# The last half gate in a bank of finished attention results, and one row of the mixed product at most behind each gate

## The chip, the cores and the metric

The kernel runs on one core of a Trainium2 chip. The metric is the device time of one execution in microseconds (us); less is better. All numbers come from runs on the chip and from the hardware profile of one execution of the kernel before.

## What is computed

Three stages stand behind each other, all in float32. The weights of the two feed-forward stages come in float64.

```python
def _attn_ref(q, k, v):                       # B, H, S, D = 4, 8, 768, 64
    for t in range(S):
        state = gamma * state + k[:, :, t] (x) v[:, :, t]
        y[:, :, t] = scale * q[:, :, t] @ state
def _moe_ref(x, w1, w2, w3, w_out):           # 3072 tokens, 512 -> 1024 -> 512
    h = (x @ w1) * (x @ w2) @ w3
    return h @ w_out
def _moe2_ref(x, w_in, w_out):                # 512 -> 2048 -> 512
    h = x @ w_in
    return (h * sigmoid(1.702 * h)) @ w_out
```

Since nothing stands between `w3` and `w_out` but a product, the kernel multiplies the two weights once (the "mixed product" `w3 @ w_out`) and applies the result to the gated values.

## The kernel before, in words

**Precision.** Each float32 operand is split into a high and a low part. ScalarE (ACT) casts the high part, VectorE (DVE) subtracts it from the value and keeps the low part. A product is then three matmuls on TensorE (PE), in `mm3`, lines 256 to 259: high by high, high by low, low by high. A "product" of 128 rows and 512 columns over 512 inputs is 12 matmuls of 512 columns.

**Weights.** `weight_steps` (lines 188 to 235) turns the float64 bits of one weight tile after the other into float32 on DVE. It is a generator: one step is one DVE instruction on 128x512 elements. A tile from 2 to 20 has ten steps: two clamps (L194), two subtractions for the low parts of the tile before (L148), two shifts (L202), two ORs (L206) and two more ORs (L216). Behind each L216, ACT casts that half's high part (`upper`, L143), and SyncE (SP) is asked for the next raw weights. Tiles from 21 have eight steps, with no low part. `magnitude` (L139, ACT) opens a tile. `work(n)` (line 243) issues n steps at that place of the program. Tiles 0 to 7 are the gate weights, 8 to 11 `w_out`, 12 to 19 `w3`, 20 to 35 the two weights of the last stage. The `w3` tiles (tag "wc", line 99) have room for two tiles, so the cast of tile 14 writes over tile 12, and so on: the high part of tile 12 + r + 2 can be written only when PE has read tile 12 + r. Each tile from 20 on, and each pair of rows of the mixed product, goes through `seven` (line 177): four TENSOR_TENSOR and three DMAs on GpSimd (POOL). The `x` buffers in which DVE prepares a tile are six halves, three tiles (line 137).

**First stage.** Attention runs in 24 chunks (`Attention.run`). Its results go to PSUM tiles `y0` and `y1`, two banks each, by turns. Between chunks, `fill` puts half gates on PE: one half of a gate product (12 matmuls) into the bank `wide`, named `psg`. Half gate 14 runs in the last chunk, half gate 15 behind attention, in the loop of lines 1026 to 1035, which takes the bank `free[halves % len(free)]`. With 15 % 5 = 0 that is the first of the list. `first_out` copies an even half gate with ACT (L1001) and multiplies an odd one into it with DVE (L1003).

**Second stage.** The loop of lines 1106 to 1136 goes over five blocks of 512 tokens (n = 1 to 5) and eight gates each (t = 0 to 7). A gate (n, t) is 24 matmuls into two banks (`psm`, six banks, so three gates). Then come, in the program's order: for t = 3 to 6 one split of the next block's input (`split_x`, ACT L272 and DVE L173), `work(...)`, the output of the gate (`gate_out`: ACT copies the first half, L299, DVE multiplies by the second, L300), and the rows of the mixed product that line 1123 lets through. A row is again 24 matmuls (`mix_mm`, two banks `psw`), followed by `work(7)` and an ACT copy (`mix_out`, L1066). In blocks 1 and 2 a pair of gates shares one buffer `h` of two, which is stored to DRAM behind the odd gate (L313); at gate (2,6) the other buffer is given to a load (line 1115), so the output of (2,6) needs the buffer whose store holds gates (2,4) and (2,5).

Each engine takes its instructions in the order in which the program issues them, so a waiting instruction holds up all that stand behind it on its engine.

Line 1123 lets a row through while the steps issued so far cover its weights. Before, that gave rows 0 and 1 behind gate (1,5), rows 2 to 4 behind (1,6) and rows 5 to 7 behind (1,7).

Of the kernel before, what the change touches and what calls it, by code (L numbers as in the profile page):

```python
# [24 lines left out]
KD, KF, KG = DM // P, DF // P, DG // P  # L25
# [20 lines left out]
def tile_kernel(  # L46
# [49 lines left out]
    WO, W3, WI = 8, 12, 20  # L96
# [21 lines left out]
    def fetch(held=False, queue=nc.sync):  # L118

        nonlocal fetched  # L120
        if fetched >= min(used + R_BUFS, 2 * len(tiles)):
            return
        i, c = divmod(fetched, 2)
        fetched += 1
        src = tiles[i][0][:, c * WC : (c + 1) * WC].bitcast(I32)
        raw = prep.tile([P, WC, 2], I32, tag="r", bufs=R_BUFS, name="raw")
        if held:
            nc.vector.memset(raw[:, :1], 0)
        queue.dma_start(raw, src.rearrange("p (c w) -> p c w", w=2))
        raws.setdefault(i, []).append(raw)  # L130

    def magnitude(i):
        if i >= len(tiles):
            return
        xs = wx.setdefault(i, [])
        for raw in raws.get(i, [])[len(xs) :]:
            x = prep.tile([P, WC], F32, tag="x", bufs=6, name="x")
            high = raw[:, :, 1].bitcast(F32)
            nc.scalar.activation(x, high, AF.Abs, scale=2.0**16)  # L139
            xs.append(x)  # L140
# [97 lines left out]
    complete = done = 0  # L238
# [4 lines left out]
    def work(n):  # L243

        nonlocal complete, done
        for _ in range(n):
            if done < limit:
                complete = next(steps, len(tiles))
                done += 1

    def weight(i):
        while complete <= i:
            work(1)
        return parts[i]
# [20 lines left out]
    def reload(key, d):  # L275
        lo = x_tiles(key)[1][:, d].bitcast(F32)
        nc.sync.dma_start(
            lo.rearrange("p (c t) -> p c t", c=CPB), xd[key][:, :, d].rearrange("c p t -> p c t")
        )

    def split_x(key, d):
        hi, lo = (t[:, d] for t in xhl[key])
        split(hi, lo, lo.bitcast(F32))

    def gate_half(t, m, key, ps):

        w = [x.rearrange("p (m k f) -> p m k f", m=2, k=KD) for x in weight(t)]
        xh, xl = xhl[key]
        for d in range(KD):
            mm3(ps, w[0][:, m, d], w[1][:, m, d], xh[:, d], xl[:, d], d == 0, d == KD - 1)  # L290
# [11 lines left out]
    def h_tile():  # L302
        return xs.tile([P, 2, TB], F32, tag="h", bufs=2, name="h")
# [562 lines left out]
    def opening(t):  # L866
        if t in range(1, 5):
            load_wm(t - 1)
        if t == 1:
            x = spare.tile([P, 7, TB], F32R, tag="ope", name="h0")  # L870
            hi2[0] = x[:, NM:]
            load_h(0, 0, NM, x[:, :NM])
        if t == KF - 2:
            for k in (0, 2):
                load_h(1, k, k + 2, prep.tile([P, 2, TB], F32R, tag="r", bufs=R_BUFS, name="h1"))
        if t in (3, 4, 5):
            split_h(0, t - 3, t - 2, hi2[0][:, t - 3 : t - 2])
        if t == 6:
            hi2["k3"] = prep.tile([P, TB], F32R, tag="x", bufs=6, name="h3")
            split_h(0, 3, 4, hi2["k3"].rearrange("p (a t) -> p a t", a=1))  # L880
        if t in (4, 6):
            split_wm(t // 2 - 2)
# [79 lines left out]
    with tc.manual_schedule():  # L962
# [4 lines left out]
        with (  # L967
            tc.tile_pool(name="p0", bufs=1, reuse_waits="tile") as p0,
            tc.tile_pool(name="ps0", bufs=1, space=PSUM, reuse_waits="tile") as ps0,
        ):  # L970
            attention = Attention(p0, ps0)
            nc.scalar.activation(still[:, :1], still[:, :1], AF.Copy, scale=0.5)
            attention.load(0)
            nc.gpsimd.dma_start(attention.mask, cmask)
            nc.sync.dma_start(attention.dv, cv)
            nc.sync.dma_start(attention.step[:, :NCK], cstep)
            attention.load(1)
            attention.factors(0)
            for c in range(2, 6):
                attention.load(c)  # L980
            for _ in range(2):
                fetch(queue=nc.gpsimd)
            attention.factors(1)
            halves = 0
            late = []
            wide = ps0.tile([P, TB], F32, name="psg")

            def first_gate(ps):
                nonlocal halves
                t, m = divmod(halves, 2)  # L990
                gate_half(t, m, 0, ps)
                late.append((t, m, ps))
                halves += 1

            def first_out(t, m, ps):
                nonlocal h
                if m == 0 and t % 2 == 0:
                    h = h_tile()
                out = h[:, t % 2]
                if m == 0:  # L1000
                    nc.scalar.copy(out, ps)  # L1001
                    return
                nc.vector.tensor_tensor(out, out, ps, ALU.mult)  # L1003
                if t % 2:
                    nc.sync.dma_start(hd[0][:, t // 2, :2], h)

            def fill(c, at):
                for _ in range((c, at) in ((6, 0), (7, 0), (8, 0))):
                    fetch(held=True)
                if at == 3 and c > 2 * CPB and halves // 2 < min(complete, KF):  # L1010
                    first_gate(wide)
                if at == 0:
                    while late:
                        first_out(*late.pop())
                if at == 1 and c in (*range(2, 6), *range(10, 14)):
                    hi, lo, x = first_x.pop(0)
                    nc.scalar.copy(hi, x)
                    engine = nc.vector if c > 2 * CPB else nc.gpsimd
                    engine.tensor_tensor(lo, x, hi.bitcast(F32), ALU.subtract)
                if c > CPB:  # L1020
                    work(PACE.get(c, (0, 1, 0, 4))[at])
                if (c, at) == (8, 2):
                    magnitude(1)

            attention.run(fill)
            free = [wide] + [
                y[:, j].rearrange("p n t -> p (n t)") for y in attention.y for j in range(2)
            ]
            while late:
                first_out(*late.pop())  # L1030
            while halves < 2 * KF:
                weight(halves // 2)
                first_gate(free[halves % len(free)])
                work(2)
                first_out(*late.pop())
        with (
# [11 lines left out]
            rows = 0  # L1048
# [57 lines left out]
            for n, i in list(enumerate(ORDER))[1:]:  # L1106
                nxt = ORDER[n + 1] if n + 1 < NB else None
                for t in range(KF):
                    if nxt is None:
                        opening(t)  # L1110
                    elif t < 2:
                        for d in range(2):
                            reload(nxt, 2 * t + d)
                    if n == 2 and t == KF - 2:
                        load_b(n, NM, nc.sync)
                    if n == 3 and t == 0:
                        load_b(n, 1, nc.sync)
                    ab = gate_mm(t, i, gate_tile)
                    if nxt is not None and t in range(KD - 1, KF - 1):
                        split_x(nxt, t - KD + 1)  # L1120
                    work(((8, 6, 3, 3)[n - 1] + (n < 4) * (t % 2)) if n < 5 else (t < 4) + (t < 5))
                    (gate_second if n > 2 else gate_first)(t, i, ab)
                    while rows < KF and (complete > W3 + rows or (n, t) == (2, KF - 1)):
                        ps = mix_mm(rows)
                        work(7)
                        mix_out(rows, ps)
                        rows += 1
                        if rows == KF:
                            stage.close()
                            pb = homes["st"] = stage.enter_context(  # L1130
                                tc.tile_pool(name="b2", bufs=1, reuse_waits="tile")
                            )
                            st_ready = [pb.tile([P, 1024], F32, tag="st", bufs=2, name="st")]
                            pb.tile([P, 2048], F32, name="gap")
                            first_g = [g_tile()]
                            first_b = [b12_tile()]
# [148 lines left out]
```

## Time and profile before

| what | value |
| --- | --- |
| median of 3 runs | 968.72 us (968.15 to 969.56) |
| the profiled execution: its own time | 968.64 us |
| its span, first to last instruction | 966.8 us |
| PE busy | 947.2 us, 98% |
| DVE busy | 705.6 us, 73% |
| ACT busy | 432.2 us, 45% |
| POOL busy | 226.8 us, 23% |
| granted TensorE clock, mean | 0.999 |
| chain that ended last, PE's share | 89% |

Busy time is the sum of an engine's instructions; matmuls overlap, so PE's share says how rarely it stands still, not how fast it is. The clock was at its upper level throughout. Time outside the span (1.8 us) is start and end of the program. The second stage of the product described above runs from 128.8 to 391 us of the span.

### The profile page before, as it was taken

The numbers are of one execution on the slowest core, as the hardware profiler recorded it, in microseconds if no ns is written. First come the engines' busy times: TensorE is split into PE (matmuls) and PEld (weight loads), VectorE is DVE, ScalarE is ACT, GpSimd is POOL, SyncE is SP. The second block draws the span as 40 slices with busy tenths as digits, with TensorE's granted clock in tenths as the row PEclk, the third lists the DMA queues.
The fourth block names the chain that finished last, engine by engine and source line by source line (L and its number), as shares of the span: only waits on it lengthen the run. The fifth ranks groups of instructions, "written<-read, shape, count | busy, mean of one in ns | idle before, by whom it ended". The sixth has DMA issues, their size and how long they took to land.

```text
span 966.8 us, 14667 instructions
## 1 busy us (share of the span) xinstructions
PE 947.2 (98%) x5656; PEld 781.6 (81%) x5656; DVE 705.6 (73%) x857; ACT 432.2 (45%) x643; POOL 226.8 (23%) x281
## 2 busy tenths in 40 slices
PE   6899999999999999999999999999999999999998
PEld 5687777888888888888888888888888888888886
DVE  5898878988899887675795776568586665566662
ACT  4554435433313212645436665556545544353430
POOL 7422100379787866240010000000000000000000
PEclk9999999999999999999999999999999999999999
DMA  9999765579998999799867845754987867766761
GB/s 351 390 356 347 279 216 197 193 243 341 343 351 318 364 322 405 281 326 340 276 227 265 307 165 219 297 207 185 324 314 279 330 230 258 253 217 231 278 230 54
DMA packets 90646, 268.52 MB, mean 278 GB/s; under 512 B 7536, under 2 KB 15984, under 8 KB 82512
## 3 DMA queue, kind: packets, MB, share of 16 engines
q1 hardware_dynamic: 74592, 188.60, 55.0%
q0 software_dynamic: 15840, 78.91, 21.3%
q8 instruction: 44, 0.72, 0.3%
q14 instruction: 26, 0.21, 0.1%
q10 hardware_dynamic: 144, 0.07, 0.0%
HBM read 166.37 MB, written 101.19 MB: 277 GB/s over the span
## 4 chain that ended last, share of the span: by engine, by line
PE 89%; DMA 4%; DVE 3%; ACT 1%; issue 1%; POOL 0%; DVEq 0%; ACTq 0%; POOLq 0%; SPq 0%
PE m L257 12%; PE m L259 12%; PE m L258 12%; PE psm L258 6%; PE psm L257 6%; PE psm L259 6%; PE a L257 4%; PE a L258 4%; PE a L259 4%; PE e L258 2%; PE e L257 2%; PE e L259 2%; DMA qkv<-in_qkv_dram 2%; PE psg L257 2%; DMA raw<-in_w_dram 1%; PE psw L259 1%
## 5 line engine op out<-in xcount | busy, mean ns | idle before, releaser
L257 PE MATMUL psm<-xh,wh 128*128 128x512 f32 x320 | 124.5, 389 | 0.0
L258 PE MATMUL psm<-xl,wh 128*128 128x512 f32 x320 | 124.5, 389 | 0.0
L259 PE MATMUL psm<-xh,wl 128*128 128x512 f32 x320 | 124.5, 389 | 0.0
L257 PE MATMUL m<-h,op 128*128 128x512 f32 x320 | 124.5, 389 | 0.0
L259 PE MATMUL m<-h,op 128*128 128x512 f32 x320 | 124.5, 389 | 0.0
L258 PE MATMUL m<-l,op 128*128 128x512 f32 x304 | 118.3, 389 | 0.0
L739 ACT CAST h<-l 128x2048 fp32r<-128x2048 f32 x38 | 72.2, 1914 | 82.3 <-PE m L259 63.7
L740 DVE TENSOR_TENSOR l<-l,h 128x2048 fp32r<-128x2048 f32 x38 | 85.4, 2285 | 17.4 <-ACT h L739 17.4
L745 POOL DMA_DIRECT2D op<-sw x6 | 3.2, 532 | 388.4 <-PE a L259 211.5
L139 ACT ACTIVATE x<-raw 128x512 f32<-128x512 f32 x72 | 46.9, 674 | 68.4 <-DMA raw<-in_wo_dram 35.6
L257 PE MATMUL a<-yh,op 128*128 128x512 f32 x192 | 74.8, 390 | 0.3 <-ACT s L611 0.3
L258 PE MATMUL a<-yl,op 128*128 128x512 f32 x192 | 74.7, 389 | 0.0
L259 PE MATMUL a<-yh,op 128*128 128x512 f32 x192 | 74.7, 389 | 0.0
L259 PEld LDWEIGHTS m<-h,op 128*128 128x128 f32 x320 | 60.1, 188 | 12.6
L259 PEld LDWEIGHTS psm<-xh,wl 128*128 128x128 f32 x320 | 60.1, 188 | 12.6
L257 PEld LDWEIGHTS psm<-xh,wh 128*128 128x128 f32 x320 | 60.1, 188 | 12.5
L257 PEld LDWEIGHTS m<-h,op 128*128 128x128 f32 x320 | 60.1, 188 | 12.4
L258 PEld LDWEIGHTS psm<-xl,wh 128*128 128x128 f32 x320 | 60.1, 188 | 12.3
L258 PEld LDWEIGHTS m<-l,op 128*128 128x128 f32 x304 | 57.1, 188 | 11.8
L257 PE MATMUL m<-h,wh 128*128 128x512 f32 x168 | 65.4, 389 | 0.0
L259 PE MATMUL m<-h,wl 128*128 128x512 f32 x168 | 65.4, 389 | 0.0
L173 DVE TENSOR_TENSOR l<-l,h 128x2048 fp32r<-128x2048 f32 x19 | 43.5, 2291 | 25.0 <-ACT h L272 23.5
(172 smaller groups left out, 2097.2 us busy)
## 6 DMA issues: line engine op xcount, KB each, us to landing
l<-gd SPq DMA_DIRECT2D x38, 1024.0 KB, 6.4
gd<-t SPq DMA_DIRECT2D x24, 1024.0 KB, 4.4
qkv<-in_qkv_dram POOLq DMA_DIRECT2D x20, 1024.0 KB, 9.0
l<-hd SPq DMA_DIRECT2D x19, 1024.0 KB, 7.9
raw<-in_w_dram SPq DMA_DIRECT2D x30, 512.0 KB, 5.7
hd<-g POOLq DMA_DIRECT2D x12, 1280.0 KB, 7.8
raw<-in_wo_dram SPq DMA_DIRECT2D x24, 512.0 KB, 7.2
gd<-g SPq DMA_DIRECT2D x24, 512.0 KB, 2.6
```

The source lines that it names most:

```text
L139: nc.scalar.activation(x, high, AF.Abs, scale=2.0**16)
L173: nc.vector.tensor_tensor(lo, x, hi.bitcast(F32), ALU.subtract)
L257: nc.tensor.matmul(ps, wh, xh, start=start, stop=False, skip_group_check=True)
L258: nc.tensor.matmul(ps, wh, xl, start=False, stop=False, skip_group_check=True)
L259: nc.tensor.matmul(ps, wl, xh, start=False, stop=stop, skip_group_check=True)
L739: nc.scalar.copy(hi, x.bitcast(F32))
L740: nc.vector.tensor_tensor(x, x.bitcast(F32), hi.bitcast(F32), ALU.subtract)
L745: queue.dma_start(t.bitcast(F32), sw[PART[name]])
```

## The change

The list `free` begins with the four banks of `y0` and `y1` and ends with `wide`. Half gate 15 takes the first entry as before, which is now the first bank of `y0`. And line 1123 decides once behind each gate whether a row fits, not again after each row, except behind gate (2,7), which would take all that are left.

```diff
             attention.run(fill)
-            free = [wide] + [
+            free = [
                 y[:, j].rearrange("p n t -> p (n t)") for y in attention.y for j in range(2)
-            ]
+            ] + [wide]
...
                     (gate_second if n > 2 else gate_first)(t, i, ab)
-                    while rows < KF and (complete > W3 + rows or (n, t) == (2, KF - 1)):
+                    last = (n, t) == (2, KF - 1)
+                    for _ in range(KF - rows if last else min(KF - rows, complete > W3 + rows)):
                         ps = mix_mm(rows)
                         work(7)
                         mix_out(rows, ps)
```

The rows 0 to 7 then stand behind the gates (1,5), (1,6), (1,7), (2,0), (2,1), (2,2), (2,3) and (2,4), one each. The number of steps issued by the end of gate (2,4) is the same as before.

On PE at the end of attention, the last matmul of half gate 14, the first two of half gate 15 and the first two of gate (1,0), in the kernel before (`psm_1827` lies in the first bank of `y0_133`; the other matmuls of half gate 15 are left out):

```order
L259 MATMUL psg_165<-xh_236,wl_1718 128x512
L257 MATMUL psg_165<-xh_236,wh_1717 128x512 [waits Activation_49]
L258 MATMUL psg_165<-xl_237,wh_1717 128x512
L257 MATMUL psm_1827<-xh_690,wh_657 128x512 [waits PE_49]
L258 MATMUL psm_1827<-xl_691,wh_657 128x512
```

And with the change:

```order
L259 MATMUL psg_165<-xh_236,wl_1718 128x512
L257 MATMUL y0_133<-xh_236,wh_1717 128x512 [waits Activation_49]
L258 MATMUL y0_133<-xl_237,wh_1717 128x512
L257 MATMUL psm_1827<-xh_690,wh_657 128x512 [waits DVE_49]
L258 MATMUL psm_1827<-xl_691,wh_657 128x512
```

Before, half gate 15 waited for ACT to copy half gate 14 out of `psg_165`. Now its wait on ACT is for an earlier cast, and gate (1,0), which writes the bank that half gate 15 used, waits on DVE for the multiplication that reads half gate 15.

On ACT, behind gate (1,6), in the kernel before (`wh_2196`, `wh_2255` and `wh_2332` are the high parts of tiles 14, 15 and 16, `psw` a row, `psm` the first half of a gate):

```order
L143 CAST wh_2196<-x_2118 128x512 [waits DVE_49]
L1066 COPY xp_2163<-psw_2165 128x2x256 [waits PE_49]
L272 CAST xh_1823<-xl_1824 128x512 [waits DMAHW7_49]
L143 CAST wh_2255<-x_2192 128x512 [waits DVE_49]
L143 CAST wh_2255<-x_2194 128x512 [waits DVE_49]
L299 COPY h_2266<-psm_2218 128x512 [waits DMAHW7_49,PE_49]
L1066 COPY xp_2301<-psw_2269 128x2x256 [waits PE_49]
L143 CAST wh_2332<-x_2251 128x512 [waits DVE_49]
L143 CAST wh_2332<-x_2253 128x512 [waits DVE_49]
```

And with the change, tiles 15 (`wh_2249`) and 16 (`wh_2306`) and, further on, 19 (`wh_2525`):

```order
L143 CAST wh_2249<-x_2195 128x512 [waits DVE_49,PE_49]
L1066 COPY xp_2163<-psw_2216 128x2x256 [waits PE_49]
L143 CAST wh_2306<-x_2245 128x512 [waits DVE_49,PE_49]
L143 CAST wh_2306<-x_2247 128x512 [waits DVE_49]
L299 COPY h_2213<-psm_2269 128x512
L1066 COPY xp_2351<-psw_2319 128x2x256 [waits PE_49]
L143 CAST wh_2525<-x_2434 128x512 [waits DVE_49,PE_49]
L143 CAST wh_2525<-x_2436 128x512 [waits DVE_49]
L1066 COPY xp_2539<-psw_2495 128x2x256 [waits DMASW7_49,DMASW0_49,Pool_49]
```

The casts of tiles 15 to 19 now wait on PE as well: for rows 1 to 5, the last readers of the buffers they write. The cast of tile 16 waits for row 2 (`psw_2319`) and stands ahead of the copy of gate (1,7) (`psm_2269`), which PE computes before row 2. In the same way the casts of tiles 17, 18 and 19 wait for rows 3, 4 and 5.

On POOL, the first of the three DMAs of each `seven`, from the second on, before (`sm0` takes pairs of rows, `sp0` to `sp3` tiles 20 to 23):

```order
L159 DMA sm0_98<-xp_2301 128x2x256
L159 DMA sm0_98<-xp_2400 128x2x256
L159 DMA sp0_89<-x_2518 128x512
L159 DMA sm0_98<-xp_2537 128x2x256
L159 DMA sp1_90<-x_2567 128x512
```

And with the change:

```order
L159 DMA sm0_98<-xp_2351 128x2x256
L159 DMA sp0_89<-x_2521 128x512
L159 DMA sm0_98<-xp_2539 128x2x256
L159 DMA sp1_90<-x_2571 128x512
L159 DMA sp2_91<-x_2623 128x512
```

Tile 20 has moved ahead of the third pair of rows, which now stands where the fourth stood; the fourth comes only behind tile 24.

## Rows read from the trace of the kernel before

**Rows 1.** The profile's page, part 1: busy time of each engine.
```profile
PE 947.2 (98%) x5656; PEld 781.6 (81%) x5656; DVE 705.6 (73%) x857; ACT 432.2 (45%) x643; POOL 226.8 (23%) x281
```

**Rows 2.** Waits of PE, whole run: us in total, times, longest us.
```profile
PE psw L259 <- DVE wl L148: 1.0, 1, 1.0
PE u L405 <- issue: 0.9, 1, 0.9
PE psg L257 <- ACT h L1001: 0.7, 1, 0.7
```

**Rows 3.** Stretches: length, busy us (instructions) of PE, PEld, DVE, ACT, POOL; clock, DMA share, GB/s.
```profile
161.00:217.00 56.00, 55.03 (x243) 45.24 (x242) 47.86 (x87) 22.97 (x40) 25.65 (x24) 1.00 0.63 212
217.00:260.00 43.00, 43.00 (x192) 35.59 (x191) 37.62 (x54) 13.83 (x24) 36.05 (x47) 1.00 0.99 343
```

**Rows 4.** Timeline of PE, last half gates: start us, duration us, instruction, idle before.
```profile
124.89 0.39 PE L259 MATMUL psg<-xh,wl 128*128 128x512 f32 x1
125.95 0.50 PE L257 MATMUL psg<-xh,wh 128*128 128x512 f32 x1 [0.68 <-ACT h L1001]
126.29 0.39 PE L258 MATMUL psg<-xl,wh 128*128 128x512 f32 x1
...
128.81 0.39 PE L257 MATMUL psm<-xh,wh 128*128 128x512 f32 x1
```

**Rows 5.** Timelines of ACT and DVE at the same place.
```profile
125.31 0.58 ACT L1001 COPY h<-psg 128x512 f32<-128x512 f32 x1 [5.55 <-PE psg L259]
129.08 0.69 DVE L1003 TENSOR_TENSOR h<-h,psg 128x512 f32<-128x512 f32 x1 [4.14 <-PE psg L259]
```

**Rows 6.** Timeline of PE, first matmul of rows and gates, 161 to 201 us.
```profile
161.45 0.39 PE L257 MATMUL psw<-wh 128*128 128x512 f32 x1
...
166.91 0.39 PE L257 MATMUL psw<-wh 128*128 128x512 f32 x1
...
168.50 0.50 PE L259 MATMUL psw<-wh,wl 128*128 128x512 f32 x1 [0.97 <-DVE wl L148]
...
173.62 0.39 PE L257 MATMUL psm<-xh,wh 128*128 128x512 f32 x1
...
195.38 0.39 PE L257 MATMUL psm<-xh,wh 128*128 128x512 f32 x1
...
200.81 0.39 PE L257 MATMUL psw<-wh 128*128 128x512 f32 x1
```

**Rows 7.** Timeline of DVE, weight steps and gate multiplications.
```profile
187.48 0.76 DVE L194 TENSOR_SCALAR x<-x 128x512 f32<-128x512 f32 x2
...
192.43 0.76 DVE L194 TENSOR_SCALAR x<-x 128x512 f32<-128x512 f32 x2
...
213.13 1.28 DVE L216 SCALAR_TENSOR_TENSOR x<-raw,x 128x512 int32<-128x512 int32 x2
...
222.84 0.69 DVE L300 TENSOR_TENSOR h<-h,psm 128x512 f32<-128x512 f32 x1 [1.41 <-PE psm L259]
...
251.81 0.69 DVE L300 TENSOR_TENSOR h<-h,psm 128x512 f32<-128x512 f32 x1
```

**Rows 8.** Timeline of ACT: casts of a weight tile; the outputs of gates (2,6), (2,7).
```profile
191.94 1.23 ACT L143 CAST wh<-x 128x512 fp32r<-128x512 f32 x2
...
259.75 1.08 ACT L299 COPY h<-psm 128x512 f32<-128x512 f32 x2 [2.24 <-DMA hd<-h]
```

**Rows 9.** Timeline of POOL: first instructions of three `seven`.
```profile
190.81 7.60 POOL L170 TENSOR_TENSOR st<-xp 128x256 f32<-128x256 f32 x1 [10.38 <-ACT xp L1066]
...
214.50 0.85 POOL L170 TENSOR_TENSOR st<-x 128x256 f32<-128x256 f32 x1 [1.63 <-DVE x L216]
...
219.59 1.28 POOL L170 TENSOR_TENSOR st<-xp 128x256 f32<-128x256 f32 x1
```

**Rows 10.** The page, part 6: stores of `h`; KB each, median us to landing.
```profile
hd<-h SPq DMA_DIRECT2D x12, 512.0 KB, 4.9
```

## The prediction

> **What bounds the kernel now.** I read the page's busy times first [rows 1]: PE is busy for 947.2 of 966.8 us, so only what PE stands still for can be gained, and only what makes it stand still can be lost. The list of PE's waits says where that is [rows 2]. Two of its lines belong to this change: 1.0 us in a row of the mixed product, for DVE's low part of a weight (L148), and 0.7 us in the last half gate, for ACT's copy out of `psg` (L1001). The stretches come third [rows 3]. From 161 to 217 us, where the rows stand, PE lacks 0.97 us and DVE is free for 8.1 of 56 us. From 217 to 260 us PE lacks nothing, but DVE is busy for 37.6 and POOL for 36.1 of 43 us. So behind the rows there is little room for DVE to make up for lost time. Then come the timelines of the places named.
>
> **The sum goes against the profiled execution**: 968.64 us, of which 966.8 are the span; the median of the runs shown is 968.72, 0.08 more. About 0.2%, 1.9 us, is what a measurement of this kernel can tell from no change.
>
> **The half gate.** Before, the last matmul of half gate 14 starts at 124.89 and half gate 15 at 125.95 [rows 4], 1.06 us later, where the usual distance is 0.23 (126.29 to 128.81 is eleven of them). The second matmul behind the pause comes after 0.34 instead of 0.23. So the wait costs 0.83 + 0.11 = 0.94 us. In the bank of `y0` it goes. But gate (1,0) writes the same bank next and must now wait for DVE to read it. In the trace DVE's multiplication starts at 129.08 [rows 5], 0.50 us behind the start of the last matmul (128.81 - 0.23 = 128.58), and takes 0.69; PE starts 0.06 after its reader has ended (ACT 125.31 + 0.58 = 125.89, PE 125.95). That is 1.25 us instead of 0.23, and 0.11 for the restart: 1.13. DVE has nothing queued ahead of that multiplication (it waited 4.14 us for it [rows 5]). **Term 1: 1.13 - 0.94 = +0.2 us.** The wait is moved, not removed.
>
> **The wait of row 1.** One block of 24 matmuls takes 5.44 us: 173.62 to 195.38 is a gate and three rows, 21.76 us, and 195.38 to 200.81 a gate [rows 6]. Row 1 took 166.91 to 173.62, 6.71. With gate (1,6) ahead of it, it starts at 161.45 + 2 x 5.44 = 172.3, while DVE had its weight ready by 168.5 [rows 6]. **Term 2: 5.44 - 6.71 = -1.3 us.** Each later row has its low parts issued 10 or more steps earlier than it needs them, so none waits there.
>
> **What the spreading does to ACT and DVE.** The `w3` buffers hold two tiles. The weights go on at nearly the pace of before, the rows no longer do, so the casts of tiles 15 to 19 must wait until PE has computed rows 1 to 5. The orders above show it: L143 waits on PE where it did not. Behind the waiting cast stand, on ACT, the copy of a gate's first half, the copy of a row and the opening of the next tile (L139); on DVE the low parts, the gate's multiplication and all further steps wait for ACT. SP's raw loads wait for DVE's L216, and POOL for tile 20. For PE this costs nothing at first: a gate's bank is needed again three gates later, which is five to six blocks of 5.44 us while rows stand between, and a cast's delay is at most two blocks. So the rows themselves run without pause. Number the blocks from row 0 at 161.45: row 5 is block 10 and ends at 161.45 + 11 x 5.44 = 221.3.
>
> But DVE loses the time. The cast of tile 19 can start 0.27 us after row 5, at 221.6 (the distance from the end of a half gate to its reader, 128.81 to 129.08 [rows 4, 5]), and one half of it takes 0.62 (two take 1.23 [rows 8]). From the low part of tile 19 to the end of tile 20, DVE has eight steps: a whole tile takes 192.43 - 187.48 = 4.95, its first pair 0.76 [rows 7], so 4.2. Tile 20 is ready at 226.4. Before, it was at 213.13 + 1.28 = 214.4 [rows 7]. **DVE is 12.0 us late**, as is POOL, which takes tile 20 from there.
>
> From here to the multiplication of gate (2,5) the two programs give DVE and POOL nearly the same work. Before, that stretch ended at 251.81 + 0.69 = 252.5, 38.1 us after tile 20, with six gate multiplications; now it has four (gates (2,0) and (2,1) lie before it), 2 x 0.69 less, and the 1.41 us that DVE then waited for PE [rows 7] go too: 38.1 - 1.4 - 1.4 = 35.3. POOL has as many `seven` in it: the third pair of rows stands where the fourth stood. So that multiplication ends at 226.4 + 35.3 = 261.7.
>
> Its end matters because of the buffer `h`: gates (2,4) and (2,5) are stored from the one that ACT needs for gate (2,6). Before, ACT's copy came at 259.75, waiting for that store [rows 8], 7.25 us after the multiplication. Now: 261.7 + 7.25 = 268.95, the copy 0.58 [rows 5], PE 0.06 later: 269.6. Gate (3,1), three gates after (2,6), needs that bank. It is block 19 and would start at 161.45 + 19 x 5.44 = 264.8. **Term 3: 4.8 + 0.1 for the restart = +4.9 us.** The same lateness holds gate (3,0) for some of it (its input's last split stands behind that multiplication), inside the same 4.9. After that a gate asks DVE for 3 or 4 steps instead of 6 or 7, so DVE catches up and I add nothing further.
>
> The bounds of term 3. Below: if DVE ran all its 41 steps and 7 other instructions undisturbed, 41 x 0.495 + 7 x 0.69 = 25.1 us, the multiplication would end at 251.5, before the 256.9 that gate (3,1) allows (264.8 - 0.06 - 0.58 - 7.25): 0. A store that lands in the median 4.9 us [rows 10] instead of 7.25 gives 2.5. Above: one POOL instruction that waits as long as the one at 190.81, 7.60 us [rows 9], where its kind takes 0.85, delays the `x` buffers and with them DVE by 6.8: 11.7. I take 4.9, since DVE, POOL and the DMA queues were as busy in the stretch that I shift as they will be.
>
> Edits that cost nothing: the reloads for block 3 come some 28 us earlier, into a stretch with a DMA share of 0.63 instead of 0.99 [rows 3]; the fourth pair of rows is stored later, but its weights are read only in block 5; the pool of block 3 opens behind row 7, at 161.45 + 15 x 5.44 = 243.1, and is first written at gate (3,0), 16 us later.
>
> **Sum: +0.2 - 1.3 + 4.9 = +3.8 us: 972.4 us.**
>
> **A rule against the change.** While DVE ran without a gap, a POOL subtraction took 7.60 us; at 214.50 the same took 0.85 [rows 9]. The Trainium skill, "SBUF — State Buffer", section "Who interferes with whom", says that a DVE instruction with two SBUF inputs and a GpSimd instruction that reads SBUF take turns at a shared port pair, and that the loser is blocked for the whole instruction. By that rule a DVE that has to catch up is the one that holds POOL up. The trace agrees at 190.81 and not at 214.50 or 219.59 (1.28), where POOL got in at once. By the rows alone it is the third rival.
>
> **Rivals.** *DVE makes it up* (0.33): between 226.4 and 256.9 us it finds the room, because it no longer waits for PE and the DMA queues, emptier before, serve it faster. The point that decides is 256.9 us for the multiplication of (2,5). For it: 41 steps alone are 20.3 us. Against it: 37.6 of 43 us were busy there before. Then +0.2 - 1.3 = -1.1: 967.5 us, not slower; with up to 3.0 us of term 3 it still is no change that can be told. *The wait is really removed* (0.04): the multiplication of half gate 15 does not hold gate (1,0), and nothing is late: -0.9 - 1.3 = -2.2, 966.4 us, faster. The order speaks against it, since the wait on DVE stands there. *POOL is locked out once* (0.11): 11.7 instead of 4.9, 979.2 us.
>
> **How the numbers follow.** The forecast, with term 3 from 3.0 to about 9 us, has 0.52. Slower by over 0.2%: 0.52 + 0.11 = 0.63, less 0.02 that I give to unknown gains; within 0.2%: 0.33; faster: 0.06. The range for 8 in 10 runs from the rival without a stall, 967.4, to term 3 at 10 us, 977.5. The likeliest case alone runs from 970.5 to 976.5.
>
> **What would show it.** In PE's waits, the lines of `psw` for DVE L148 and of `psg` for ACT L1001 are gone; a line of `psm` for DVE L1003 of about 1 us is there, and one of `psm` for ACT's L299 or DVE's L173 of 4 to 5 us in all, between 259 and 271 us. ACT's L143 waits for rows of `psw`; DVE is free for more than 15 us from 178 to 222 us. The first `seven` of tile 20 starts near 226 us, the multiplication of (2,5) ends near 262. The prediction is wrong if that multiplication ends before 257, or if PE stands still between rows.

## The result and the profile after

The changed kernel takes 977.06 us (median of five runs, 975.87 to 977.47), beside 968.15 us for the kernel before on the same chip (967.62 to 969.56): a ratio of 1.0081, 95% interval 1.0068 to 1.0094, or 6.6 to 9.1 us more. The forecast was 972.4. The sign and the mechanism are right, and the size is less than half of what came: 3.8 us were expected, 8.9 measured. The time lies inside the stated range of 967.4 to 977.5 us, close to its upper end. The profiled execution has a span of 975.3 us, against 966.8.

PE's waits in the changed kernel (us in total, times, longest) answer to [rows 2]:

```profile
PE psm L257 <- ACT h L299: 3.8, 2, 3.5
...
PE psm L257 <- DVE h L1003: 0.9, 1, 0.9
...
PE psm L258 <- DVE xl L173: 0.3, 1, 0.3
```

The two lines that the change was to take away, `psw` for DVE L148 and `psg` for ACT L1001, are gone. In their place stand 0.9 us for DVE's L1003 and 3.8 us for ACT's copies of gates (L299). The stretches (PE, PEld, DVE, ACT and POOL busy, then granted clock, DMA share, GB/s) answer to [rows 3]:

```profile
161.00:217.00 56.00, 56.00 (x249) 46.39 (x248) 40.54 (x74) 19.86 (x36) 8.79 (x11) 1.00 0.56 180
217.00:260.00 43.00, 43.00 (x192) 35.61 (x191) 39.06 (x57) 13.16 (x23) 31.75 (x41) 1.00 0.82 269
260.00:300.00 40.00, 36.19 (x147) 29.01 (x146) 33.84 (x47) 10.27 (x19) 35.63 (x46) 0.91 0.97 346
```

While the rows stand, PE has no gap left (56.00 of 56, before 55.03), and DVE has 40.5 us of work instead of 47.9. The work that DVE did not do there is missing later: between 260 and 300 us PE stands still for 3.8 us, and the mean granted clock is 0.91. Two starts in PE's timeline date the loss, that of row 0 and that of the blend's first matmul (`m`). The kernel before:

```profile
161.45 0.39 PE L257 MATMUL psw<-wh 128*128 128x512 f32 x1
...
391.21 0.39 PE L257 MATMUL m<-h,wh 128*128 128x512 f32 x1
```

The changed kernel:

```profile
163.19 0.39 PE L257 MATMUL psw<-wh 128*128 128x512 f32 x1
...
399.67 0.39 PE L257 MATMUL m<-h,wh 128*128 128x512 f32 x1
```

From row 0 to the blend it is 236.48 us instead of 229.76: +6.72. All of it is in by then; the span ends 8.5 us later, as the blend starts 8.5 us later. Row 0 itself is 1.74 us late, of which 1.53 arose ahead of half gate 9 (its first matmul at 96.40 instead of 94.87). That part is not put down to the change: in the profiled executions of this study, which have the same code up to there, that matmul starts between 94.4 and 97.2 us, and in the changed kernel's the granted clock was at 0.50 from 42 to 44 us, ahead of any changed code. The remaining 0.21 is the half gate. So the trace holds 0.21 + 6.72 = 6.9 us of the change's own, inside the interval above.

**Where DVE lost its time** is in the waits between 161 and 224 us:

```profile
ACT wh L143 <- PE psw L258: 32.7, 5, 8.1
DVE wl L148 <- ACT wh L143: 12.2, 4, 4.8
```

Five casts wait for rows (tiles 15 to 19), and DVE waits for four of them, 12.2 us. **Where PE paid** is in the timelines of ACT and of PE:

```profile
259.35 0.68 ACT L139 ACTIVATE x<-raw 128x512 f32<-128x512 f32 x1 [1.93 <-DMA sp<-x]
263.59 0.67 ACT L139 ACTIVATE x<-raw 128x512 f32<-128x512 f32 x1 [3.56 <-DVE x L216]
264.16 0.57 ACT L299 COPY h<-psm 128x512 f32<-128x512 f32 x1
```

```profile
260.89 0.39 PE L259 MATMUL psm<-xh,wl 128*128 128x512 f32 x1
264.78 0.79 PE L257 MATMUL psm<-xh,wh 128*128 128x512 f32 x1 [3.51 <-ACT h L299]
265.37 0.63 PE L258 MATMUL psm<-xl,wh 128*128 128x512 f32 x1
265.80 0.63 PE L259 MATMUL psm<-xh,wl 128*128 128x512 f32 x1
...
270.07 0.61 PE L257 MATMUL psm<-xh,wh 128*128 128x512 f32 x1
270.49 0.42 PE L258 MATMUL psm<-xl,wh 128*128 128x512 f32 x1
270.75 0.40 PE L259 MATMUL psm<-xh,wl 128*128 128x512 f32 x1
```

The matmul at 264.78 is gate (3,0), which needs the bank that ACT's copy of gate (2,5) sets free. That copy (264.16) stands behind the L139 at 263.59. The row names DVE, one of whose steps had just ended; but ACT passed its wait for DMAs only at 263.54, and the one that landed last, at 263.48, was the load of the raw weights that this L139 reads. In the kernel before, the same L139 stands ahead of the same copy, and there the row says so:

```profile
250.63 0.68 ACT L139 ACTIVATE x<-raw 128x512 f32<-128x512 f32 x1 [2.47 <-DMA raw<-in_wi_dram]
```

The load is issued by SP as soon as DVE's L216 has freed its buffer. In the changed kernel:

```profile
257.03 0.33 SPq L129 DMA_DIRECT2D raw<-in_wi_dram  x1
```

It lands after 6.45 us. In the kernel before it was issued at 244.42 and landed after 6.11 us. From row 0 the issue is 93.84 instead of 82.97 us away, 10.9 us late, as DVE is. So DVE's lateness reaches PE through a load: L216, the load, L139, the copy, the bank.

Then something comes that no term of the prediction held: behind the pause a matmul starts every 0.43 us instead of every 0.23. The windows show why, in the column of the granted clock:

```profile
262.00:264.00 2.00, 0.00 (x0) 0.00 (x0) 2.00 (x3) 0.41 (x1) 2.00 (x4) 0.93 0.78 315
264.00:266.00 2.00, 1.22 (x3) 1.03 (x4) 1.65 (x5) 1.38 (x4) 1.90 (x3) 0.50 1.06 264
266.00:268.00 2.00, 2.00 (x7) 1.51 (x6) 2.00 (x4) 0.55 (x1) 2.00 (x3) 0.50 0.85 277
268.00:270.00 2.00, 2.00 (x6) 1.58 (x5) 2.00 (x3) 0.68 (x1) 2.00 (x4) 0.50 0.99 377
270.00:272.00 2.00, 2.00 (x9) 1.58 (x8) 1.02 (x2) 0.00 (x0) 1.90 (x3) 0.87 1.04 424
```

The clock is at 0.50 (1.2 GHz) from 264 to 270 us. PE's busy time reads 2.00 of 2 there, so a busy PE hides this loss; only the clock and the count (6 or 7 matmuls instead of 11) show it.

The ledger, each start against the usual 0.227: the pause 264.78 - 260.89 - 0.23 = 3.66; fourteen starts at the low clock, 270.75 - 264.78 - 14 x 0.227 = 2.79; three short waits at 273.50, 306.39 and 314.74 with their restarts, 0.56, 0.20 and 0.60. Together 7.8. The trace has 6.72, and with the 1.3 us that row 1 gives back 8.0.

### The profile page after: what moved, and what is told of

Same layout as the page of the kernel before. It is cut to its first block, busy times and chain, and to the rows that moved or that the text cites. A ratio compares the mean times of both kernels' runs of the same rounds, so it can differ in the third digit from the quotient of the medians.

```text
span 975.3 us, 14663 instructions
## 1 busy us (share of the span) xinstructions
PE 952.6 (98%) x5656; PEld 785.1 (80%) x5656; DVE 711.2 (73%) x857; ACT 431.3 (44%) x643; POOL 220.1 (23%) x281
## 4 chain that ended last, share of the span: by engine, by line
PE 85%; DMA 6%; DVE 4%; POOL 2%; issue 2%; ACT 1%; DVEq 0%; ACTq 0%; POOLq 0%; SPq 0%
PE m L258 12%; PE m L257 12%; PE m L259 12%; PE psm L258 5%; PE psm L257 5%; PE psm L259 5%; PE a L257 4%; PE a L258 4%; PE a L259 4%; DMA qkv<-in_qkv_dram 3%; PE e L258 2%; PE e L257 2%; PE e L259 2%; PE psg L257 2%; DMA raw<-in_wo_dram 1%
## 5 line engine op out<-in xcount | busy, mean ns | idle before, releaser
L740 DVE TENSOR_TENSOR l<-l,h 128x2048 fp32r<-128x2048 f32 x38 | 85.4, 2285 | 17.5 <-ACT h L739 17.4
L139 ACT ACTIVATE x<-raw 128x512 f32<-128x512 f32 x72 | 47.1, 676 | 95.7 <-DMA raw<-in_wo_dram 46.0
L206 DVE SCALAR_TENSOR_TENSOR x<-raw,x 128x512 int32<-128x512 int32 x72 | 63.2, 910 | 0.0
```

The source lines that it names most:

```text
L206: nc.vector.scalar_tensor_tensor(bits, raw[:, :, 0], 29, bits, ALU.logical_shift_right, ALU.bitwise_or)
L740: nc.vector.tensor_tensor(x, x.bitcast(F32), hi.bitcast(F32), ALU.subtract)
```

## The experiments

All are measured in five rounds beside the kernel before. "Row 0 to blend" is the distance between the two starts above; "gate to row 0" is from the first matmul of half gate 9 to row 0, 66.58 us before and 66.79 in the changed kernel.

**The two edits apart.** The bank alone (new list `free`, old loop), and the rows alone (old list, new loop):

> The bank alone: the last half gate goes to the first bank of y0, the rows stand as before. The theory (the wait is moved to gate (1,0), not removed): 0.0 to +0.3 us against before, a line psm <- DVE L1003 of about 0.9 us and none of psg <- ACT L1001. The rival (the wait is removed): -0.9 us. A second rival (the bank itself costs the 8 us): +8 us.

> The rows alone: at most one row behind each gate, the last half gate in psg as before. The theory (the whole loss comes from spreading the rows past the casts' two buffers): +6.5 to +9 us against before, PE idle for 3 to 4 us before gate (3,0) and the granted clock at 0.5 for some us behind it. The rival (bank and rows are needed together, or the loss lies in the first stage): within 2 us of before.

The rows alone: 975.96 against 968.25 us, ratio 1.0082 (1.0068 to 1.0096), row 0 to blend +7.0, a pause of 3.9 us at (3,0) with the clock at 0.50 behind it. The whole loss lies in the rows. The bank alone: 967.60 against 968.25, ratio 0.9990 (0.9981 to 0.9999), a little faster than the theory allowed. Up to row 0 the theory holds: PE waits 0.85 us for DVE L1003, gate to row 0 is 66.79, +0.21. But row 1's wait then shrinks:

```profile
PE psw L259 <- DVE wl L148: 0.2, 1, 0.2
```

Before it was 1.0 [rows 2]. With the wait behind the half gate instead of ahead of it, DVE gets that half gate earlier than PE goes on, and in its row of steps the low part of row 1's weight ends 0.8 us earlier against row 0 (168.44 - 161.65 = 6.79 us behind it, before 169.04 - 161.45 = 7.59). Row 0 to blend is 0.75 us shorter.

**Which bank.** Two other places for the half gate, old loop:

```
-            free = [wide] + [y0[:, 0], y0[:, 1], y1[:, 0], y1[:, 1]]
+            free = [y0[:, 1], y0[:, 0], y1[:, 1], y1[:, 0], wide]   # e3_bank3
+            free = [y1[:, 0], y1[:, 1], y0[:, 0], y0[:, 1], wide]   # e5_y1
```

> The last half gate in the second bank of y0, which gate (1,0) does not write (gate (1,1) does, for its second half, some 10 us later); the rows as before. If the order of the banks decides, as the theory says, PE waits neither for ACT L1001 nor for DVE L1003, and the time is 0.7 to 1.0 us below before. The rival (PE is held there by something else, such as the gate's input or weight): no change, and another line in PE's waits at 126 to 130 us.

> The last half gate in the first bank of the other tile, y1, the rows as before. The theory is now that a gate's bank waits for the readers of the whole two-bank tile y0, not of its own bank: y1 is needed only by gate (1,2), 10.9 us after gate (1,0), so neither ACT L1001 nor DVE L1003 holds PE, and the time is 0.6 to 1.2 us below before. The rival (gate (1,0) needs the last half gate's multiplication whatever bank it stands in): PE waits 0.85 us for DVE L1003 as in the two runs before this one, time 0 to 0.6 us below before.

The other bank of `y0`: 968.30 against 968.25, ratio 1.0001 (0.9993 to 1.0010), and the wait stands as it stood:

```profile
128.57 0.50 PE L257 MATMUL psm<-xh,wh 128*128 128x512 f32 x1 [0.85 <-DVE h L1003]
```

Gate (1,0) begins in the first bank, and still waits at its first matmul. So the program's wait goes by the tile of two banks, not by the bank (the kernel opens its pools with `reuse_waits="tile"`); the expectation was wrong. Row 0 to blend is 0.71 us shorter here too. So this trace and that of the bank alone agree, while their ratios are 1.0001 and 0.9990: 0.1% is not told apart here. In `y1` the half gate holds nobody: no line for L1001 nor for L1003, gate to row 0 65.61 (-0.97). Row 1's wait stays (0.8 us), and row 0 to blend is only 0.15 us shorter. The time is 967.61 against 968.16, ratio 0.9992 (0.9983 to 1.0000): 0.55 us less, where 0.6 to 1.2 were expected, and not clear of no change.

**How far the rows are spread.** Only row 1 moved behind (1,6), with the half gate in `y1`; and, with the old bank, at most two rows behind a gate (1, 2, 2, 2, 1 came out):

```
                     while rows < KF and (...):
+                        if (n, t, rows) == (1, 5, 1):
+                            break                                      # e6_y1row
-                    while rows < KF and (...):
+                    for _ in range(min(2, KF - rows, max(0, complete - W3 - rows))):   # e11_cap2
```

> The last half gate in y1, and of the rows only row 1 moved, behind gate (1,6) instead of (1,5); rows 2 to 7 keep their places. The theory: both waits go and no cast is delayed, since row 5 stands where it stood: 1.6 to 2.6 us below before, no line of psw for DVE L148 and DVE as early at tile 20 as before (about 213 to 214 us). The rival (one row fewer behind (1,5) already delays the casts): 0 to 8 us above before, with ACT L143 waiting for psw.

> The kernel before, with at most two rows behind each gate: 1, 2, 2, 2, 1 behind (1,5) to (2,1), so row 5 ends two blocks (10.9 us) earlier than in the changed kernel; the bank as before. The theory (the loss comes from the cast of tile 19, which waits for row 5): tile 20 is ready within 2 us of before, no pause at (3,0), and the time is 0.5 to 1.5 us below before, since row 1's wait goes. The rival (any spreading of the rows costs, in proportion): 3 to 5 us above before.

Row 1 alone, with the half gate in `y1`: 966.73 against 968.16, ratio 0.9982 (0.9973 to 0.9991); gate to row 0 -0.97, row 0 to blend -1.28, PE without a gap from 161 to 400 us. It has the lowest median of the study; the 1.4 us gained are a little less than the 1.6 expected at the least. One cast waits 1.5 us for a row, and DVE loses 0.2 us by it. Two rows at most: 967.62 against 968.44, ratio 0.9993 (0.9984 to 1.0001), not clear of no change, row 0 to blend also -1.28. There three casts wait for rows and DVE loses 5.5 us to them:

```profile
ACT wh L143 <- PE psw L258: 8.7, 3, 3.7
DVE wl L148 <- ACT wh L143: 5.5, 3, 2.6
```

Measured from row 0, DVE ends tile 20 after 52.96 us in the kernel before, 56.15 here and 64.84 in the changed kernel (L216 at 213.13, 216.94 and 226.75, each with its 1.28, less the start of row 0). A DVE that is 3.2 us late (the theory allowed 2) costs PE nothing, one that is 11.9 us late costs 8. So the price does not go in proportion. The prediction's 4.4 us of slack (256.9 against 252.5) lie between the two; no run lies closer to that point.

**Can the lost time be put off?** In the changed kernel: fewer steps behind the late gates of block 2, the rest in later blocks, in two forms; a third `h` buffer for (2,6) and (2,7); a gate's copy, multiplication and store ahead of the steps, without and with that buffer.

```
-                    work(((8, 6, 3, 3)[n - 1] + (n < 4) * (t % 2)) if n < 5 else (t < 4) + (t < 5))
+                    work((3 if n == 2 and t > 1 else (8, 6, 4, 4)[n - 1] + t % 2) if ...)       # e4_fewer
+                    work((4 if n == 2 and 1 < t < 6 else (8, 6, 3, 3)[n - 1] + t % 2) if n < 5
+                         else (t < 4) + (t < 5) + (t < 6))                                      # e7_later
-            h = h_tile()
+            h = third_h.pop() if third_h and (i, t) == (ORDER[2], KF - 2) else h_tile()         # e8, e10
...
                     ab = gate_mm(t, i, gate_tile)
+                    early_out = n == 2 and t > 1
+                    if early_out:
+                        gate_first(t, i, ab)                                                    # e9, e10
...
-                    (gate_second if n > 2 else gate_first)(t, i, ab)
+                    if not early_out:
+                        (gate_second if n > 2 else gate_first)(t, i, ab)                        # e9, e10
```

> The changed kernel with fewer steps of weight work behind the gates of block 2 from (2,2) on (3 instead of 6 or 7; 20 of the 21 steps go to blocks 3 and 4). The theory (DVE is late and has the steps ahead of the gate's multiplication): 11 to 14 steps of 0.5 to 0.65 us less stand ahead of the multiplication of (2,5), it ends 6 to 9 us earlier, PE does not stand still at (3,0) or (3,1), the clock does not fall there, and the time is 0.5 to 2 us below before. The rival (the store of h or the DMA queues hold the gates whatever DVE does): 5 to 9 us above before, as the changed kernel.

> The changed kernel with 4 steps instead of 6 or 7 behind gates (2,2) to (2,5), and the ten steps made up behind gates of blocks 4 and 5. The theory (DVE's lost 12 us, not the number of rows, is the price): the multiplication of (2,5) ends 5 to 7 us earlier than in the changed kernel, PE waits under 1.5 us at (3,0) and (3,1), the clock stays at 1.00 there, and the time is between 1.5 us below and 2 us above before. The rival (the 12 us come due wherever the steps stand, as the end of the gates showed where 20 steps were moved): another wait behind 300 us and 3 to 10 us above before.

> The changed kernel with a third buffer h for gates (2,6) and (2,7), so that ACT's copy of (2,6) no longer waits for a store of h. The step of the prediction (that copy, 7.25 us behind the multiplication of (2,5), holds gate (3,1)) expects 0 to 3 us above before. The theory from the trace (ACT's copy of (2,5) is late behind an L139 that waits for DVE, and holds gate (3,0) before the store matters): the pause at (3,0) stays at 3 to 4 us, and only the short wait at (3,1) goes, 6 to 9 us above before.

> The changed kernel; behind gates (2,2) to (2,7) the gate's copy, multiplication and store of h are issued ahead of the split of x and the weight steps instead of behind them. The number of steps is the same. The theory (the steps that stand ahead of a late gate's copy and multiplication hold PE): the copy and the multiplication of (2,5) come 4 to 5 us earlier, PE waits under 1 us at (3,0) and under 2 us at (3,1), and the time is between 1 us below and 2.5 us above before. The rival (the lost 12 us of DVE come due all the same, as where steps were put off): 4 us or more above before, with a wait at another place.

> The same with the third buffer h for (2,6) and (2,7). The theory: no wait for ACT L299 between 259 and 275 us, the granted clock stays at 1.00, and the time is within 1.5 us of before. The rival: as for the run before it, 4 us or more above before.

None of them beats the kernel before. Fewer steps: 980.83 against 968.25, ratio 1.0125 (1.0109 to 1.0140); steps later: 985.77 against 968.16, 1.0184 (1.0157 to 1.0210), with runs from 982.8 to 990.8. In both the pause at (3,0) is gone, as the theory said (PE busy 40.00 of 40 us from 260 to 300). But the steps come due later. With fewer steps:

```profile
300.00:350.00 50.00, 48.88 (x216) 40.17 (x214) 49.50 (x59) 12.88 (x23) 43.68 (x50) 1.00 0.95 349
350.00:400.00 50.00, 44.27 (x194) 36.35 (x194) 37.02 (x42) 10.93 (x19) 35.85 (x38) 0.99 0.87 321
```

DVE is busy for 49.5 of 50 us from 300 to 350, and at the end of the gates PE stands still, for a DVE that itself waits for a load of `h`:

```profile
PE m L257 <- DVE g L300: 9.7, 1, 9.7
```

```profile
DVE g L1089 <- DMA h<-hd: 8.0, 1, 8.0
```

(7.7 and 5.0 us where ten steps were moved.) POOL issues that load at 393.35, behind a `seven` that waited for DVE's steps until 381.72; in the kernel before it went out at 376.17. So the late steps are paid through POOL's queue and a load, not by DVE's own work at that place. The time of the theory was wrong in both. The rival written for the second run, that the lost time comes due wherever the steps stand, holds in kind, and at a higher price than it named.

The third `h` buffer: 974.16 against 968.16, ratio 1.0056 (1.0043 to 1.0070), row 0 to blend +4.0 instead of +6.7. The pause at (3,0) stays, 3.4 us, and the short waits behind it go. So the store of `h` accounts for the small part, and ACT's late copy for the large one (here the L139 ahead of it starts when a store of a weight tile, `sp<-x`, has landed, at 262.95). Of the 2.7 us, 1.4 are the short waits and 1.2 lie in the clock, which was low for a shorter time (eleven starts, 268.67 - 264.56 - 11 x 0.227 = 1.6 us):

```profile
264.23 0.50 PE L257 MATMUL psm<-xh,wh 128*128 128x512 f32 x1 [3.38 <-ACT h L299]
264.56 0.39 PE L258 MATMUL psm<-xl,wh 128*128 128x512 f32 x1
264.79 0.39 PE L259 MATMUL psm<-xh,wl 128*128 128x512 f32 x1
265.02 0.55 PE L257 MATMUL psm<-xh,wh 128*128 128x512 f32 x1
265.37 0.63 PE L258 MATMUL psm<-xl,wh 128*128 128x512 f32 x1
```

Output first: 975.92 against 968.44, ratio 1.0082 (1.0069 to 1.0095), and with the third buffer 977.00, 1.0085 (1.0072 to 1.0098). The bank no longer holds gate (3,0); its input does, since the split of x now stands behind a copy that waits:

```profile
PE psm L257 <- ACT xh L272: 6.1, 1, 6.1
```

With the third buffer this wait is 3.3 us, and one of 4.6 for a copy of (3,·) follows at 288.73; that profile is of the slowest of six executions (982.14 us). Each time PE waits for an ACT that has waited for DMAs: in the first kernel for a load of raw weights (issued at 256.43, landing after 7.0 us) and then for the store of `h` (2.13 us), in the second for stores of weight tiles (`sp<-x`, 2.40 and 13.16 us). As the rival had it, the time is lost at another place; that a late DVE stands behind each of these DMAs is not shown. These two runs moved the split as well as the output, so they do not test the output's place by itself.

**The price of a pause.** The kernel before, with one pause put in where nothing is late:

```
+                    if (n, t) == (5, 2):
+                        for x in (xhl[i][0], xhl[i][0][:, :3]):
+                            nc.scalar.copy(x, x.bitcast(F32))
                     ab = gate_mm(t, i, gate_tile)
```

> The kernel before with a pause put in ahead of gate (5,2), near 358 us: ACT copies seven of the eight 512-column pieces of two passes over that gate's xh onto themselves (estimate 3.5 to 4 us from 0.62 us for one piece), and PE must wait for it. Nothing else there is late. The theory (the pause itself brings the clock down): the granted clock falls to 0.50 for 3 to 6 us behind the pause, and the time is 5 to 7 us above before. The rival (the clock fell in the changed kernel for another reason than the pause): the clock stays at 1.00 and the time is 3.5 to 4.2 us above before.

974.67 against 968.44 us, ratio 1.0067 (1.0055 to 1.0079): 5.3 to 7.7 us for a pause of 361.90 - 358.02 - 0.23 = 3.65. PE and the windows:

```profile
358.02 0.39 PE L259 MATMUL psm<-xh,wl 128*128 128x512 f32 x1
361.90 0.80 PE L257 MATMUL psm<-xh,wh 128*128 128x512 f32 x1 [3.49 <-ACT xh L1120]
362.50 0.63 PE L258 MATMUL psm<-xl,wh 128*128 128x512 f32 x1
...
364.63 0.46 PE L257 MATMUL psm<-xh,wh 128*128 128x512 f32 x1
364.92 0.39 PE L258 MATMUL psm<-xl,wh 128*128 128x512 f32 x1
```

```profile
360.00:362.00 2.00, 0.10 (x1) 0.10 (x1) 2.00 (x2) 1.97 (x3) 1.92 (x2) 0.84 1.03 377
362.00:364.00 2.00, 2.00 (x5) 1.61 (x6) 1.29 (x1) 0.99 (x2) 1.70 (x3) 0.50 1.05 440
364.00:366.00 2.00, 2.00 (x8) 1.59 (x8) 0.00 (x0) 0.00 (x0) 1.90 (x4) 0.81 0.94 390
```

The clock falls, as the theory said; the low clock lasts some 3 us here and costs 364.92 - 361.90 - 7 x 0.227 = 1.4 us. Row 0 to blend is 5.27 us longer. So here, behind gates and rows that kept PE busy without a gap from 170 us on, the pause by itself is enough; no lateness of the other engines is needed.

## Why the prediction was right in sign and short in size

**Term 1, the half gate (+0.2): right in its sum, wrong in its reason.** The trace has +0.21. The wait belongs to the whole tile `y0`, not to the bank, as the run with the other bank shows. What it did not see is that the moved wait lets DVE run ahead, which in the old order of the rows gives back 0.75 us. In the changed kernel row 1 no longer waits, so nothing of this was left to gain.

**Term 2, row 1 (-1.3): right.** Row 0 to blend is 1.28 us shorter in both kernels that move row 1 and do not stall.

**Term 3, DVE's lateness (+4.9): the mechanism right, the size off; it measured 8.0.** The first link held to a tenth: tile 20 was forecast 12.0 us late and is 11.9 late, and POOL's first subtraction starts 64.93 us behind row 0 (228.12 - 163.19), forecast 64.95. DVE was free for 44 - 27.86 = 16.1 us from 178 to 222. Three links behind it failed.

**DVE's recovery.** From tile 20 to the multiplication of (2,5) I took 35.3 us, 2.8 less than before. It took 265.45 - 228.03 = 37.4, only 0.7 less. The two multiplications went (1.4 us), and DVE stood still for 0.8 us instead of 2.9, but its steps and splits took 2.9 us longer. One line of DVE's steps in that stretch (count, busy us, mean ns), in the kernel before and in the changed one:

```profile
L216 DVE SCALAR_TENSOR_TENSOR x<-raw,x 128x512 int32<-128x512 int32 x11 | 8.2, 778 | 0.0
```

```profile
L216 DVE SCALAR_TENSOR_TENSOR x<-raw,x 128x512 int32<-128x512 int32 x11 | 10.1, 951 | 0.0
```

That is 11 x 0.173 = 1.9 of these 2.9 us. Single steps take 1.2 us instead of 0.68 while POOL subtracts; DVE's and POOL's timelines in the changed kernel:

```profile
261.14 1.21 DVE L206 SCALAR_TENSOR_TENSOR x<-raw,x 128x512 int32<-128x512 int32 x1
```

```profile
260.63 1.17 POOL L170 TENSOR_TENSOR st<-x 128x256 f32<-128x256 f32 x1
261.76 1.17 POOL L170 TENSOR_TENSOR st<-x,st 128x256 f32<-128x256 f32 x1
```

The Trainium skill, "SBUF — State Buffer", section "Who interferes with whom", says that a DVE instruction with two inputs in SBUF and a POOL instruction that reads SBUF hold each other up. The rows agree in kind, and here both pay, not POOL alone as the prediction had it. My third rival had POOL locked out for long; its first subtraction on tile 20 took 0.73 us, so that did not happen here. In the two kernels with the output first the same subtraction took 3.66, with fewer or later steps 4.27 and 5.20.

**Which gate waits, and for what.** I let gate (3,1) wait for the store of `h`, and gave (3,0) a share inside that. Gate (3,0) waited first, for ACT's copy of (2,5), because an L139 that waited for a load of raw weights stood ahead of it in ACT's queue: 3.66 us. The prediction names this link (SP's raw loads wait for DVE's L216, and the copy stands behind L139) and gives it no term. What I reckoned for (3,1) shrank to the wait at 273.50, and with two later ones to 1.36 us. The third `h` buffer takes these away and leaves the pause. All these waits of PE come to 3.66 + 1.36 = 5.0 us, beside the 4.9 of the term. That they agree is luck: the multiplication of (2,5) came 2.0 us later against row 0 than forecast (102.26 instead of 100.25), and most of the wait was another gate's, for something else.

**The clock.** I priced the pause at its length. It cost 2.79 us more, in fourteen starts at the lower level of the clock (1.2 GHz). This is the largest of the three, and nearly the whole distance from 4.9 to 8.0. The range reached to 10 us for this term, on account of a longer wait; it holds, but not for the reason that it was drawn for.

The rivals: that DVE makes it up fell for this spread and held for the smaller one (3.2 us late, no pause). That the wait is really removed is false for `y0` and true for `y1`.

## What to carry to other kernels

Spreading work of PE more evenly moves the moment at which its operands' buffers come free. Where a buffer holds two tiles, count which producer then waits for which consumer, and ask whether that producer's engine has the slack to make the time up before the next bound stretch; here 3.2 us passed unseen and 11.9 us cost 8, and neither of the two later places tried for the work was free. Follow a late engine's buffers to the loads that wait for them, and further to whoever waits for the loads. Price a pause of some 3.5 us in a stretch where PE is busy throughout at more than its length, and read the granted clock behind it, since the busy time does not show it. And a small edit that moves only what waits (row 1 behind one more gate, the half gate in a tile that nobody needs soon) took both waits away and gained 1.4 us (0.9 to 2.6).

## What the runs showed of the hardware

Behind pauses of 3.4 to 3.9 us PE came back at a granted clock of 0.50, in the four kernels that had one such pause and no longer one (waits of 3.38, 3.49, 3.51 and 3.89 us; behind the first, three matmuls ran at full speed before it fell). It came back at 0.50 behind the longer waits of the other runs too (6.14, 7.73 and 9.65 us), and fell to 0.50 within 2 us behind waits of 2.40 us (at 352 us, ten steps moved), 3.27 and 4.56 us (output first with the third buffer). Length alone does not decide: in the first stage the clock stayed at 1.00 behind a wait of 2.32 us that ended at 58.35 (output first with the third buffer; PE had been busy for 2.00 of 2 us from 54 to 56), and in the changed kernel it was at 0.50 from 42 to 44 us behind one of 1.49 us that ended at 40.56 (PE busy for 1.06 of 2 us from 38 to 40 and for 1.14 of 2 from 40 to 42). Behind the waits of 0.85 us at the half gate the starts stayed 0.23 apart. The low clock lasted from 3 to 6 us and cost 1.4, 1.6 and 2.8 us where it is worked out above; what sets the length within that range was not tried. The Trainium skill, "TensorE: Matmul & The Clock Gate", section "Wait — 56ns, not 53.3ns?", gives 426.7 ns from start to start at the low clock and 215.7 ns at the high one for 512 columns. The rows agree with the first (0.43) and have 0.227 for the second.
